# Induced-set attention and squared-ReLU MLP on one core: scores read in a burst, batch 0 transposed on TensorE, the weights' chain in one PSUM bank

## The chip, the cores and the metric

The kernel runs on one core of a Trainium2 chip. The metric is the time of one execution in microseconds (us); of several runs the median counts. PE is TensorE (matmuls; PEld its weight loads), DVE is VectorE, ACT is ScalarE, POOL is GpSimd, and SP issues the DMAs. Each engine works through its own instructions in the order that was fixed when the program was built, and waits in place for what an instruction needs.

## What is computed

```python
x: (4, 12480, 128); inducing: (32, 128); w_in: (128, 2048); w_out: (2048, 128)   # weights arrive as float64
def mab(q, kv):
    s = scale * (q @ kv.T);  a = softmax(s, -1);  return a @ kv
h = mab(inducing, x)          # 32 rows look at all 12480 rows of a batch
y = mab(x, h)                 # 12480 rows look at the 32 rows of h
out = relu(y @ w_in) ** 2 @ w_out
```

## The kernel before

Four batches (b = 0 to 3) of 12480 rows are each cut into seven groups G (six of 1920 rows, one of 960) and into 26 chunks of 480 rows; four chunks make a group. All tiles hold features or the 32 inducing rows on partitions.

**First attention, `first(b)`.** For each group, `scores` (L264) multiplies the transposed rows `xp` (loaded from `xT` by `load_xT`, L259) with the inducing rows into PSUM; DVE scales them into `sT` and keeps the maximum (L298). When all seven groups are there, a global maximum is made (L305 to L316), ACT takes the exponential (L323), DVE transposes it 32x32-wise into `en` (L333), and PE multiplies `en` with the rows themselves, `xnb`, loaded from `xn` in halves of a group (L283 to L287), into `hacc` (L345). Every group has its own `hacc` in PSUM, which DVE adds into `hq` (L351, L353). Two small matmuls (L360, L361) and L363 to L365 give `hT`, the 32 attended rows.

**Second attention, `second(b, G)`.** `scores` again, now with `hT`; DVE transposes out of PSUM into `e` (L381) and takes the maximum (L383), POOL subtracts it (L387), ACT takes the exponential (L388), DVE sums (L391 to L393), POOL divides (L394), DVE transposes back (L397), and the weights `a` are written as two halves of float16 to DRAM (`ad`, L408) and loaded back in another layout as `dT` (L428). `squares(b, G)` (L442 to L454) makes 32 further squared features, which land in rows 96 to 127 of `dT` (`zz`, four DMAs a group).

**The MLP by pairs.** Each row of y is a mix of 32 rows of h, so relu(y @ w_in) squared is written with 512 squared differences of the mixing weights. `Chunk.up` (L638) multiplies `dT` with the constant `pairs` into `hp`, `lift` squares it on ACT (L647) into `g`, `down` multiplies `g` with the batch's weights `w16` (L653) and `dT` with `lin` (L654) into `po`, and `o = po * osc + bias` goes out on ACT (L657) or DVE (L659), whichever has less work held against it (`to_act`), and by DMA to `outT` (L660). Three `o` tiles exist.

**The weights of a batch, `prepare(b)`.** A chain from `hT`: `hw` = h @ w_in, some forty small DVE operations, `products(c)` (DVE, L518, four tiles G) and `sums(c)` (16 matmuls each, L527; evacuated into `w16` by ACT, L175, or DVE, L179), `R` (L534), `cat` (L580 to L582), `w4` (L606, into `lin`). Each of its PSUM results takes the one buffer of `side_psum`, so that each waits until the one before has been read. The four `sums` must all be evacuated before the first chunk of the batch can be finished.

**The start.** The weights are read as pairs of 32-bit words and made float32 on DVE by `narrow` (L236 to L242): `w_in` in four pieces of seven operations, then `w_out` in four (`wo`, L224). Between them stand the first attention of batch 0, `prepare(0)` with `second(0, 0)` and `second(0, 1)`; then the chunks begin.

**Order.** During the chunks a list `plan` says at which chunk each step of the next batches' generators is recorded: `spread(gen, steps, start, length)`, with constants (`PACE`, `MOST`, `EARLY`, `LONG`, `LAG`, `WEIGHTS`). `background(k)` runs what is due. The framework then moves instructions on each engine by a model of its own; what stands in the program is shown below under the change. The pool of `xp` tiles has NX = 9 buffers, that of `xnb` XB = 5, the PSUM of scores and squares (`att_psum`) and of the chain (`side_psum`) one each. A fallback behind `tc.If` at the end is not executed.

## Time and profile before

| | us |
|---|---|
| median of 3 runs (lowest to highest) | 462.41 (461.12 to 466.04) |
| the profiled execution | 464.73 |
| its span | 463.0 |
| first chunk's `hp` on PE | 86.1 |
| last ACT square of the last chunk | 454.5 |

The span runs from the first to the last instruction of the profiled execution. The profile gives busy time per engine; a window view gives the same for any stretch, in order: length, PE, PEld, DVE, ACT, POOL (each busy us and number of instructions), granted TensorE clock, share of the DMA engines, GB/s. A window view of one line gives that line's engine alone. The timeline gives start, duration, engine, line, output <- inputs and count of merged instructions, and in brackets the engine's idle time before with what released it. "The chain that ended last" goes back from the last instruction to what released each step. A float32 matmul stands as two in the trace (x8 for four), a float32 transpose through PE as one. Weight loads show stationary shapes as 128\*32.

### The profile page before, as it was taken

The numbers are of one execution on the slowest core, as the hardware profiler recorded it, in microseconds if no ns is written. First come the engines' busy times: TensorE is split into PE (matmuls) and PEld (weight loads), VectorE is DVE, ScalarE is ACT, GpSimd is POOL, SyncE is SP. The second block draws the span as 40 slices with busy tenths as digits, with TensorE's granted clock in tenths as the row PEclk, the third lists the DMA queues.
The fourth block names the chain that finished last, engine by engine and source line by source line (L and its number), as shares of the span: only waits on it lengthen the run. The fifth ranks groups of instructions, "written<-read, shape, count | busy, mean of one in ns | idle before, by whom it ended". The sixth has DMA issues, their size and how long they took to land.

```text
span 463.0 us, 8566 instructions
## 1 busy us (share of the span) xinstructions
PE 366.8 (79%) x2979; PEld 163.2 (35%) x2979; DVE 325.7 (70%) x902; ACT 282.0 (61%) x397; POOL 85.9 (19%) x93
## 2 busy tenths in 40 slices
PE   0644744899979889878789888988879898788994
PEld 0003413543335333333244234433433344343441
DVE  8969378685643199497561899689626999996442
ACT  1004123479994497437567798566666878067993
POOL 1000011141210030232200132144100423340000
PEclk9999975699979799799599999999999999999998
DMA  7999980377759983667889958644794354337432
GB/s 296 421 248 392 372 295 24 97 240 249 207 173 337 335 277 101 197 188 187 266 276 293 344 195 244 195 138 145 240 290 154 102 167 165 101 128 231 151 136 105
DMA packets 64771, 100.71 MB, mean 218 GB/s; under 512 B 22992, under 2 KB 53968, under 8 KB 64720
## 3 DMA queue, kind: packets, MB, share of 16 engines
q1 hardware_dynamic: 64720, 100.09, 66.3%
q8 instruction: 25, 0.41, 0.4%
q14 instruction: 26, 0.21, 0.1%
HBM read 64.91 MB, written 31.95 MB: 209 GB/s over the span
## 4 chain that ended last, share of the span: by engine, by line
PE 30%; DVE 28%; DMA 26%; ACT 6%; issue 5%; SPq 2%; POOL 1%; ACTq 0%; DVEq 0%; POOLq 0%
DMA xnb<-xn_dram 8%; PE hp L638 8%; PE po L653 7%; ACT g L647 5%; DMA outT_dram<-o 5%; PE s L264 4%; PE hacc L345 4%; DMA xp_False<-xT_dram 4%; DMA dT<-zz 3%; DVE o L659 3%; DVE G L518 3%; DVE a L407 2%; PE wq L527 2%; DMA wo<-w_out_dram 2%; DMA dT<-ad 2%
## 5 line engine op out<-in xcount | busy, mean ns | idle before, releaser
L647 ACT ACTIVATE g<-hp 128x960 f16<-128x960 f32 x208 | 194.4, 974 | 60.7 <-PE hp L638 48.2
L638 PE MATMUL hp<-dT,pairs 96*128 96x480 f16 x416 | 121.4, 381 | 7.3 <-ACT g L647 4.9
L653 PE MATMUL po<-g,w 128*128 128x480 f16 x416 | 115.8, 377 | 7.6 <-ACT o L657 3.4
L387 POOL TENSOR_TENSOR e<-e,mx 128x480 f32<-128x480 f32 (+1 forms) x28 | 28.0, 999 | 232.2 <-DVE mx L383 76.3
L659 DVE TENSOR_SCALAR o<-po,osc,bias 128x480 f32<-128x480 f32 x60 | 45.4, 763 | 30.5 <-PE po L654 17.8
L653 PEld LDWEIGHTS <-w 128*128 128x128 f16 x416 | 40.6, 100 | 60.7 <-issue 19.3
L638 PEld LDWEIGHTS <-pairs 96*128 96x128 f16 x416 | 35.8, 101 | 66.6 <-issue 42.1
L345 PE MATMUL hacc<-xnb,en 128*32 128x128 f32 x784 | 38.3, 324 | 16.8 <-DMA xnb<-xn_dram 8.7
L264 PE MATMUL s<-xp_False,indT_sb 128*32 128x480 f32 (+1 forms) x224 | 32.9, 665 | 22.4 <-DMA xp_False<-xT_dram 12.1
L654 PE MATMUL po<-dT,lin 128*128 128x480 f16 x104 | 39.1, 379 | 7.7 <-DMA dT<-zz 7.5
L452 POOL TENSOR_TENSOR zz<-z 128x480 f16<-128x480 f32 (+1 forms) x28 | 30.2, 1078 | 66.3 <-DVE z L448 39.8
L323 ACT ACTIVATE sT<-sT,nb 128x480 f32<-128x480 f32 (+1 forms) x28 | 18.2, 658 | 33.5 <-DVE nb L316 33.5
L394 POOL TENSOR_TENSOR e<-e,z 128x480 f32<-128x480 f32 (+1 forms) x28 | 27.0, 967 | 56.1 <-DVE z L393 36.9
L345 PEld LDWEIGHTS hacc<-xnb,en 128*32 128x32 f32 x784 | 24.4, 126 | 33.6 <-DMA xnb<-xn_dram 9.7
L657 ACT ACTIVATE o<-po,bias,osc 128x480 f32<-128x480 f32 x44 | 33.0, 762 | 5.2 <-DMA outT_dram<-o 4.4
L353 DVE TENSOR_TENSOR hq<-hacc,hq 128x128 f32<-128x128 f32 x24 | 7.0, 291 | 37.6 <-PE hacc L345 37.6
L264 PE MATMUL s<-xp_False,hT 128*32 128x480 f32 (+1 forms) x224 | 27.7, 563 | 4.3 <-DVE k L195 1.4
L448 DVE TENSOR_SCALAR z<-sq,off,cut 128x480 f32<-128x480 f32 (+1 forms) x28 | 21.5, 767 | 9.3 <-PE sq L442 9.3
L518 DVE TENSOR_TENSOR G<-hwp,hw 128x512 f16<-128x512 f16 x64 | 24.9, 455 | 4.1 <-PE wq L527 4.1
L388 ACT ACTIVATE e<-e 128x480 f32<-128x480 f32 (+1 forms) x28 | 16.2, 578 | 17.0 <-POOL e L387 17.0
L404 ACT ACTIVATE a<-a,lessen 128x480 f16<-128x480 f32 (+1 forms) x20 | 13.6, 681 | 16.5 <-DVE a L397 16.3
L298 DVE TENSOR_SCALAR_CACHE_REDUCE sT<-s 128x480 f32<-128x480 f32 (+1 forms) x28 | 17.0, 608 | 9.1 <-PE s L264 9.1
(190 smaller groups left out, 419.2 us busy)
## 6 DMA issues: line engine op xcount, KB each, us to landing
outT_dram<-o SPq DMA_DIRECT2D x104, 240.0 KB, 2.8
xp_False<-xT_dram SPq DMA_DIRECT2D x24, 960.0 KB, 6.8
xnb<-xn_dram SPq DMA_DIRECT2D x28, 448.0 KB, 5.2
xnb<-xn_dram SPq DMA_DIRECT2D x24, 512.0 KB, 5.9
dT<-ad SPq DMA_DIRECT2D x72, 120.0 KB, 2.6
ad<-a SPq DMA_DIRECT2D x24, 240.0 KB, 2.5
dT<-zz SPq DMA_DIRECT2D x104, 30.0 KB, 2.3
wi<-w_in_dram SPq DMA_DIRECT2D x4, 512.0 KB, 5.6
```

What stands on the lines that cost most here:

```text
L264: nc.tensor.matmul(ps[32 * q:32 * q + 32, 0:w], lhsT, xp[:, w * q:w * q + w], start=True, stop=True,)
L345: st.last = nc.tensor.matmul(hacc[32 * q:32 * q + 32, 0:P], en[:, t], xg[:, t % 8], start=t < 4, stop=t + 4 >= nb32,)
L387: nc.gpsimd.tensor_tensor(e[:, 0:t], e[:, 0:t], mx[:, 0:t].unsqueeze(2).broadcast_to([P, t, MI]), op=ALU.subtract)
L394: nc.gpsimd.tensor_tensor(e[:, 0:t], e[:, 0:t], z[:, 0:t].unsqueeze(2).broadcast_to([P, t, MI]), op=ALU.mult)
L452: nc.gpsimd.tensor_tensor(g[rows], zv[rows], zv[rows], op=ALU.mult)
L518: tt(g[:, :, MI * j:MI * j + n], hwp[:, :, 0:n], hw16f[:, :, s0:s0 + n], op=ALU.mult)
L638: nc.tensor.matmul(hp[:, i, 0:CH].rearrange("p (q t) -> p q t", q=4), pairs[0:96, (2 * j + i) * P:(2 * j + i + 1) * P], self.dT[0:96], sta ...
L647: nc.scalar.activation(self.g[:, 2 * j:2 * j + 2], self.hp.pop(j)[:, 0:2, 0:CH], AF.Square)
L653: nc.tensor.matmul(po[:, 0:CH], st.w16[:, i], self.g[:, i], start=i == 0, stop=False)
L654: done = [nc.tensor.matmul(po[:, 0:CH].rearrange("p (q t) -> p q t", q=4), st.lin, self.dT, start=False, stop=True)]
L657: nc.scalar.activation(o, po[:, 0:CH], AF.Identity, bias=st.bias, scale=st.osc)
L659: done.append(nc.vector.tensor_scalar(o, po[:, 0:CH], st.osc, st.bias, op0=ALU.mult, op1=ALU.add))
```

## The change

Nothing in the results is changed. There are five parts.

1. **Batch 0 is read once.** `xT` of batch 0 is no longer loaded. All 13 halves of batch 0's rows are loaded at the start into five `xnb` tiles, four slices of a new tile `scored`, two G tiles and two tiles of the start pool. `turn(G)` transposes each 128x128 block on PE against `ident` into `two_banks` PSUM (15 blocks a group), and ACT copies the halves into the `xp` tile. The same halves serve `hacc`. `words` has 4 buffers instead of 6.
2. **One `hacc` per batch.** PE sums all groups in one PSUM bank; the six adds into `hq` go.
3. **The second scores in a burst.** `second` writes its transposed scores into one of eight slots of `scored` and yields right after; the plan runs this first step of all groups close together (`READ`), the other steps at their own pace (`REST`). The following batch's `xp` loads are due right after the reads (`NX` 9 to 7), and its `first` and `prepare` are due earlier (batch 3's `head` 53.6 chunks instead of 61, batch 1's 10.8 instead of 13.9).
4. **The weights' chain** uses one `bank` of PSUM in slices, its small matmuls are regrouped, all four `sums` go side by side into one `wq`, are evacuated by ACT alone, and one reduction takes their maximum. `w4` comes ahead of the sums. `prepare_w_out` and the squares use the `po` pool.
5. **Batch 0's later groups** (2 to 6) are read in the start; their further steps are held behind the mark `bias` of `prepare(0)`. Evacuation of `o`: on ACT for the 18 chunks after each `head` (`heavy`) and the last chunk, on DVE otherwise (66 on ACT and 38 on DVE, before 44 and 60).

```diff
-NX = 9
+NX = 7
+HEAVY = 18
-MOST = 17
-PACE = (1.2, 2, 2, 3)
-EARLY = -1
+SLOTS = 8
+READ = (0, 2, 1, 1)
+REST = 2.6
...
+        def turn(G):
+            w = WID[G]
+            xp = st.xp[G] = flow.tile([P, 4 * CH], F32, tag="xp", name=f"xp_{b}_{G}", bufs=NX)[:, 0:4 * w]
+            to = xp.rearrange("p (q n) -> p q n", q=4)
+            for h in range(2 * G, min(2 * G + 2, HALVES)):
+                k = 8 - h % 2
+                ps = two_banks(f"xt_{h}").rearrange("p a (t c) -> p (a t) c", c=P)
+                for t in range(k):
+                    nc.tensor.transpose(ps[:, t], xns[h][:, t], ident)
+                whole = k if h < HALVES - 1 else 7
+                c0 = 256 * (h % 2)
+                nc.scalar.copy(
+                    to[:, :, c0:c0 + 32 * whole].rearrange("p q (t r) -> p t q r", r=32),
+                    ps[:, 0:whole].rearrange("p t (q r) -> p t q r", q=4),
+                )
...
-            hacc = side_psum(f"hacc_{b}_{G}")
+            hacc = hacc or side_psum(f"hacc_{b}")
...
-            if G == 0:
+            if G == NG - 1:
                 nc.vector.tensor_copy(hq[:, 0:P], hacc[:, 0:P])
-            else:
-                nc.vector.tensor_tensor(hq[:, 0:P], hacc[:, 0:P], hq[:, 0:P], op=ALU.add)
...
-        e = work.tile([P, 15, MI], F32, tag="e2", name=f"e2_{b}_{G}")
+            k = 480 * ((NG * b + G) % SLOTS)
+            e = scored[:, k:k + 480].rearrange("p (t i) -> p t i", i=MI)
         nc.vector.transpose(ef[:, 0:wb], ps[:, 0:wb])
+        yield
...
-            ps = side_psum(f"wq_{b}_{c}")
             for k in range(NF):
-                nc.tensor.matmul(ps[:, 0:P], g[:, k], w_hi[:, k], start=k == 0, stop=k == NF - 1)
-            evac(st.w16[:, c], ps[:, 0:P], P, tsg[:, c:c + 1])
-            nc.vector.tensor_reduce(wm[:, c:c + 1], ps[:, 0:P], axis=AX.X, op=ALU.max, apply_absolute_value=True)
+                last = nc.tensor.matmul(wq[:, c * P:c * P + P], g[:, k], w_hi[:, k], start=k == 0, stop=k == NF - 1)
+            nc.scalar.mul(st.w16[:, c], wq[:, c * P:c * P + P], tsg[:, c:c + 1])
...
-    for G in range(NG):
-        sts[0].xp[G] = load_xT(0, G)
+    sts[0].rows = {h: load_half(0, h, homes[h]) for h in range(HALVES)}
...
             for G in range(NG):
-                free = max(0, G + NG - NX)
-                start = max(reads[b - 1, free] + 0.6, EARLY if b == 1 else -9)
+                start = reads[b - 1, G] + 0.4
                 spread(loads(b, G), 1, start, 0)
-                spread(sums, 1, start + 3, 0)
-            start += 3.5
+                start = max(start + 2.5, 26 * (b - 2) + 7 + 1.4 * G)
+                spread(sums, 1, start, 0)
+            start += 1
             spread(sums, 18, start, LONG)
-            head = max(start + LONG + LAG, 26 * b - MOST)
+            head = max(start + LONG + LAG, 26 * (b - 1) + 0.6)
             spread(prepare(b), 19, head, WEIGHTS)
...
-                spread(second(b, G), 4, reads[b, G], 2)
+                spread(gen, 1, reads[b, G], 0)
+                spread(gen if b else behind(gen, lambda: sts[0].marks), 4, rest, 2)
...
-                done = chunks[n - 1].down()
+                done += chunks[n - 1].down(heavy(n - 1))
```

**PE at the very start.** `s_0_G` are the first scores of batch 0's group G, `xt` the transposed blocks, `place` and `rows` further homes of the halves. Before:

```order
L264 MATMUL s_0_0_220<-xp_0_False,indT_sb 32x480 x4
L264 MATMUL s_0_1_236<-xp_1_False,indT_sb 32x480 x4
L264 MATMUL s_0_2_242<-xp_2_False,indT_sb 32x480 x4
L264 MATMUL s_0_3_258<-xp_3_False,indT_sb 32x480 x4
L264 MATMUL s_0_4_264<-xp_4_False,indT_sb 32x480 x4
L264 MATMUL s_0_5_290<-xp_5_False,indT_sb 32x480 x4
L264 MATMUL s_0_6_296<-xp_6_False,indT_sb 32x240 x4
```

and now:

```order
L302 MATMUL xt_230<-ident,xnb_164 128x128 x8
L302 MATMUL xt_240<-ident,xnb_165 128x128 x7
L302 MATMUL xt_266<-ident,xnb_166 128x128 x8
L278 MATMUL s_0_0_249<-xp_0_229,indT_sb 32x480 x4
L302 MATMUL xt_276<-ident,xnb_167 128x128 x7
L302 MATMUL xt_292<-ident,xnb_168 128x128 x8
L278 MATMUL s_0_1_285<-xp_1_265,indT_sb 32x480 x4
L302 MATMUL xt_302<-ident,scored 128x128 x7
L302 MATMUL xt_328<-ident,scored 128x128 x8
L278 MATMUL s_0_2_311<-xp_2_291,indT_sb 32x480 x4
```

Each group's scores now stand behind 15 transposes, one half ahead of the scores that need them.

**DVE between the last `en` tiles and `hT` of batch 0.** `no` is the narrowing of `w_out`. Before:

```order
L333 STREAM_TRANSPOSE en_4_455<-sT_217 128x480
L353 TENSOR_TENSOR hq_332<-hacc_3_432,hq_332 128x128
L333 STREAM_TRANSPOSE en_5_475<-sT_217 128x480
L353 TENSOR_TENSOR hq_332<-hacc_4_458,hq_332 128x128
L333 STREAM_TRANSPOSE en_6_494<-sT_217 128x256
L272 MEMSET sT_967 128x16
L353 TENSOR_TENSOR hq_332<-hacc_5_477,hq_332 128x128
L353 TENSOR_TENSOR hq_332<-hacc_6_496,hq_332 128x128
L363 TENSOR_SCALAR zr_512<-hs_509 128x32
```

and now:

```order
L243 TENSOR_SCALAR no_m<-wo_394 128x512
L357 STREAM_TRANSPOSE en_4_572<-sT_226 128x480
L244 SCALAR_TENSOR_TENSOR wo_sb<-no_m,no_r 128x512
L357 STREAM_TRANSPOSE en_5_590<-sT_226 128x480
L357 STREAM_TRANSPOSE en_6_607<-sT_226 128x256
L286 MEMSET sT_1004 128x16
L375 COPY hq_468<-hacc_482 128x128
L197 TENSOR_SCALAR inv_t<-wsum 128x1
```

No operation of DVE stands between the `en` tiles any more that waits for PE; one copy of the whole sum follows the last.

**DVE at the change from batch 2 to batch 3.** Before, from the `bias` of batch 3 (chunk 78 is its first; `w_1_151` is its `w16`, `o_0`, `o_1` are its first outputs):

```order
L518 TENSOR_TENSOR G_2_4187<-hwp_4032,hw_3_3959 128x16x32 x4
L406 TENSOR_SCALAR a_3_3_4484<-a_3_3_4482,lessen 128x480
L529 TENSOR_REDUCE wm_4034<-wq_0_4168 128x1
L381 STREAM_TRANSPOSE e_3_4_4543<-s_3_4_4538 128x480
L407 SCALAR_TENSOR_TENSOR a_3_3_4484<-a_3_3_4482,lessen,a_3_3_4484 128x480
L410 TENSOR_TENSOR least_d<-least_d,a_3_3_4484 128x480
L383 TENSOR_REDUCE mx_3_4_4545<-e_3_4_4543 128x15
L179 TENSOR_SCALAR w_1_151<-wq_1_4201,tsg 128x128
...
L179 TENSOR_SCALAR w_1_151<-wq_3_4322,tsg 128x128
...
L659 TENSOR_SCALAR o_0_4706<-po_0_4700,osc_157,bias_158 128x480
```

and now (`o_21` to `o_25` are the last outputs of batch 2):

```order
L683 TENSOR_SCALAR o_21_4626<-po_21_4620,osc_146,bias_147 128x480
L544 TENSOR_TENSOR G_2_4078<-hwp_3872,hw_3_3803 128x16x32 x4
L433 SCALAR_TENSOR_TENSOR a_3_6_4550<-a_3_6_4548,lessen,a_3_6_4550 128x240
L436 TENSOR_TENSOR least_d<-least_d,a_3_6_4550 128x240
L683 TENSOR_SCALAR o_22_4644<-po_22_4638,osc_146,bias_147 128x480
L732 TENSOR_REDUCE dmin<-least_d 128x1
L544 TENSOR_TENSOR G_3_4118<-hwp_3872,hw_3_3803 128x16x32 x3
...
L683 TENSOR_SCALAR o_25_4715<-po_25_4709,osc_146,bias_147 128x480
...
L683 TENSOR_SCALAR o_0_4733<-po_0_4727,osc_157,bias_158 128x480
```

The last products and the last group's weights of batch 3 stood between outputs of batch 2 and of batch 3; now they stand four chunks ahead of the end of batch 2. At the change from batch 0 to batch 1 the four sums still stand on PE among the first four `hp` of batch 1, as before, but four of the seven second scores of batch 1 that stood among them stand ahead of them now.

More of the change, by code (lines that the diff above doesn't have):

```diff
@@ L293, in first @@
                 xns = {h: load_xn(h) for h in range(XB)}
+            if not b:
+                turn(G)
             ps = att_psum(f"s1_{b}_{G}")
@@ L301, in first @@
             yield
-        xns = xns or {h: load_xn(h) for h in range(XB)}
         m1 = small("m1")
@@ L536, in prepare @@
             )
-        cat = st.cat
-        rm = small("rm")
-        nc.vector.tensor_reduce(rm, ps[:, 0:P], axis=AX.X, op=ALU.max, apply_absolute_value=True)
-        nc.vector.tensor_copy(cat[:, 0:P], ps[:, 0:P])
-        yield
-        products(0)
-        products(1)
-        bp = side_psum(f"pl_{b}")
-        nc.tensor.matmul(bp[:, 0:1], before, inc[:, NF - 1:NF], start=True, stop=True)
-        nc.tensor.matmul(bp[0:1, 2:3], inc[:, NF - 1:NF], onec[:, 0:1], start=True, stop=True)
-        nc.tensor.matmul(bp[:, 4:5], every, rm, start=True, stop=True)
         pl, tl, t = small("pl"), small("tl"), small("t")
@@ L554, in prepare @@
         ts(flags[:, b:b + 1], bp[0:1, 2:3], MX + 0.5, None, op0=ALU.is_le)
+        yield
+        bp2 = bank[:, 136:152]
+        for k in range(NF):
+            q = k % 4
+            nc.tensor.matmul(
+                bp2[32 * q:32 * q + 32, 0:MX], hws[:, k], hot[:, k], start=k < 4, stop=k >= NF - 4,
+            )
+        cat = st.cat
+        rm = small("rm")
+        nc.vector.tensor_reduce(rm, ps[:, 0:P], axis=AX.X, op=ALU.max, apply_absolute_value=True)
+        nc.vector.tensor_copy(cat[:, 0:P], ps[:, 0:P])
+        nc.vector.tensor_copy(cat[:, P + 16:P + MI], bp2[:, 0:MX])
+        cs = work.tile([P, 4, MI], F32, tag="cs", name=f"cs_{b}")
+        nc.vector.tensor_copy(cs, cat[:, P:P + MI].unsqueeze(1).broadcast_to([P, 4, MI]))
+        yield
+        nc.tensor.matmul(bp[:, 4:5], every, rm, start=True, stop=True)
+        ps = bank[:, 160:424]
+        rep4 = rep.rearrange("p q i -> p (q i)")
+        nc.tensor.matmul(ps[0:96, 0:P + MI], rep4[:, 0:96], cat, start=True, stop=True)
+        nc.tensor.matmul(ps[:, 256:257], cs.rearrange("p j r -> p (j r)"), part, start=True, stop=True)
+        nc.tensor.matmul(ps[:, 260:261], cat[:, 0:P], onec[:, 0:1], start=True, stop=True)
         ts(tl, bp[:, 4:5], 2.0 ** -60, None, op0=ALU.max)
@@ L603, in prepare @@
         nc.scalar.copy(g4[:, :, 16:MI], hot)
-        ps = side_psum(f"w4_{b}")
         for k in range(NF):
-            nc.tensor.matmul(ps[96:P, 0:P], g4[:, k], w_hi[:, k], start=k == 0, stop=k == NF - 1)
-        ts(st.lin[96:P], ps[96:P, 0:P], t[96:P], None, op0=ALU.mult)
+            nc.tensor.matmul(bank[96:P, 0:P], g4[:, k], w_hi[:, k], start=k == 0, stop=k == NF - 1)
+        ts(st.lin[96:P], bank[96:P, 0:P], t[96:P], None, op0=ALU.mult)
+        products(1)
+        wq = side_psum(f"wq_{b}")
+        sums(0)
         yield
+        products(2)
+        sums(1)
+        yield
+        products(3)
         sums(2)
         yield
-        sums(3)
-        nc.vector.tensor_reduce(cm2[:, 1:2], wm, axis=AX.X, op=ALU.max)
+        last = sums(3)
+        st.ends = last, nc.vector.tensor_reduce(cm2[:, 1:2], wq, axis=AX.X, op=ALU.max, apply_absolute_value=True)
         ts(cm2[:, 1:2], cm2[:, 1:2], inv_t, None, op0=ALU.mult)
@@ L708, in smallest, with heavy @@
         yield
-    plan = []
+    plan, busy = [], []
+    def heavy(n):
+        return any(a <= n < z for a, z in busy)
     def spread(gen, steps, start, length):
@@ L714, in spread, with behind @@
             plan.append((start + length * n / steps, len(plan), gen))
+    def behind(gen, marks):
+        while True:
+            with ExitStack() as held_back:
+                for i in marks():
+                    held_back.enter_context(tc.issue_after(i.ins))
+                if next(gen, gen) is gen:
+                    return
+            yield
     def loads(b, G):
@@ L753, in background @@
             due = next(todo, None)
-    soon = chain(second(0, 0), second(0, 1))
+    soon = chain(scored_by[0, 0], scored_by[0, 1])
     for n, _ in enumerate(prepare(0)):
-        if n == 3:
+        if n == 0:
             prepare_w_out()
@@ L769, in attend_then_relu2_mlp @@
         for j in (0, 1):
-            chunk.lift(j)
+            done = [chunk.lift(j)]
             if nxt:
```

111 lines of the change are left out of this document (57 added, 54 removed).

## The prediction

> **What bounds the kernel now.** I read the busy times, then the chain that ended last, then windows.
>
> ```profile
> PE 366.8 (79%) x2979; PEld 163.2 (35%) x2979; DVE 325.7 (70%) x902; ACT 282.0 (61%) x397; POOL 85.9 (19%) x93
> 8.19 17.83 DMA xp_False<-xT_dram
> 38.54 9.12 DMA xnb<-xn_dram
> 59.62 1.11 PE hw L264 x8
> 86.15 1.71 PE hp L638 x4
> ```
>
> No engine is full over the whole. The chain (last four rows) shows three stages: until 59.6 us transfers and DVE make batch 0's `hT`; until 86.2 the weights' chain runs and no chunk does; then 104 chunks. In the third stage I count ACT's squares, two to a chunk, per stretch (first number in parentheses), and look at the engines where they stop:
>
> ```profile
> 190.00:200.00 10.00, 4.32 (x5) 0.80 0.56 165
> 200.00:210.00 10.00, 0.00 (x0) 1.00 0.54 164
> 380.00:390.00 10.00, 8.59 (x10) 1.00 0.43 138
> 390.00:400.00 10.00, 2.46 (x3) 0.83 0.55 174
> 400.00:410.00 10.00, 1.83 (x2) 1.00 0.28 75
> 410.00:420.00 10.00, 8.53 (x10) 1.00 0.51 166
> 440.00:450.00 10.00, 9.89 (x12) 1.00 0.39 139
> 330.00:350.00 20.00, 16.80 (x191) 8.11 (x182) 6.58 (x17) 12.23 (x15) 0.00 (x0) 1.00 0.94 299
> 360.00:390.00 30.00, 27.37 (x203) 12.02 (x202) 30.00 (x79) 24.60 (x32) 9.37 (x9) 1.00 0.40 126
> 390.00:410.00 20.00, 15.27 (x142) 7.94 (x141) 18.90 (x53) 5.92 (x9) 7.10 (x8) 0.91 0.41 125
> ```
>
> Undisturbed at the end, 12 squares pass in 10 us. At 200 to 210 none passes, at 390 to 410 five. These are the changes to batch 1 and batch 3: the new batch's first outputs wait for its four sums, and these for DVE, which is 18.9 of 20 us busy with the batch's products and last groups. Sixty us earlier (330 to 350) DVE was busy 6.58 of 20. So the chunks' stage is bound by work that comes at the wrong time, PE being next to full elsewhere.
>
> **The change part by part.** *The start.* Its end was set by DVE:
>
> ```profile
> 8.82 0.42 DVE L236 TENSOR_SCALAR ni_a<-wi 128x512 uint32<-128x512 uint32 x1
> 12.62 0.42 DVE L236 TENSOR_SCALAR ni_a<-wi 128x512 uint32<-128x512 uint32 x1
> 31.60 0.40 DVE L298 TENSOR_SCALAR_CACHE_REDUCE sT<-s 128x240 f32<-128x240 f32 x1
> 47.71 1.07 PE L345 MATMUL hacc<-xnb,en 128*32 128x128 f32 x14 [2.76 <-DMA xnb<-xn_dram]
> 54.02 0.43 DVE L333 STREAM_TRANSPOSE en<-sT 128x256 f32<-128x256 f32 x1
> 59.37 0.19 DVE L365 TENSOR_TENSOR hT<-hs,zr 128x32 f32<-128x32 f32 x1
> ```
>
> One `narrow` takes 3.8 us (first two rows). From the last scores (32.0) to `hT` (59.6) passed 27.6 us, with DVE waiting for `hacc`, which waited for rows. Now the rows lie there. Between the last scores and `hT` the new DVE order has 3.2 narrowings (12.2), seven `en` (six of 0.67 and 0.43: 4.5) and small operations (1.3), 18 us, then the last `hacc`, one copy, two small matmuls and three operations (2.8, from 56.6 to 59.4 before): 20.8. If the last scores are in at 32 again, `hT` is there at 52.8 instead of 59.6: 6.8 earlier. Whether they are is up to PE:
>
> ```profile
> 12.11 1.83 PE L264 MATMUL s<-xp_False,indT_sb 128*32 128x480 f32 x8 [12.11 <-DMA xp_False<-xT_dram]
> 60.50 0.99 PE L264 MATMUL s<-xp_False,hT 128*32 128x480 f32 x8
> 58.09 0.30 PEld L360 LDWEIGHTS hs<-z,every 128*128 128x128 f32 x2 [0.89 <-DVE hq L353]
> 75.00 0.50 PEld L546 LDWEIGHTS pl<-inc,before 128*128 128x128 f32 x2 [2.53 <-issue]
> L617 PE MATMUL cm<-ident,cm 128*1 128x128 f32 x12 | 2.4, 271 | 0.0
> 99.53 0.49 PE L617 MATMUL cm<-ident,cm 128*1 128x128 f32 x3
> ```
>
> The same scores take 1.83 us early and 0.99 later; PE runs at half speed at the start (the clock column, which reads 1.00 there, does not show it) and had sped up by 58 us, after ten us of dense `hacc`. No 128x128 block is transposed before. Its weight load is like one of L360 or L546: 0.15 us fast, 0.25 slow; the matmul behind it adds 0.11 ((0.49 - 0.27) / 2) if loads overlap it, and its whole 0.27 if nothing overlaps. So a block costs 0.15 to 0.52, 98 blocks 15 to 51 us. I take 0.15 from the second group on, since PE has no gap any more: a group is 15 x 0.15 + 0.99 = 3.2 us, and six and a half groups from 10 us on, the first two at 5.6 (15 x 0.25 + 1.83), end at 10 + 11.2 + 4.5 x 3.2 = 36: 4 later than before. ACT's 13 copies of up to 1024 columns (like L647, 974 ns for 960) fill 13 of some 26 us.
>
> ```profile
> 60.00:75.00 15.00, 5.86 (x60) 2.60 (x53) 13.72 (x49) 5.42 (x8) 2.17 (x2) 0.65 0.49 177
> 75.00:90.00 15.00, 9.91 (x94) 6.78 (x95) 9.90 (x40) 4.79 (x8) 2.94 (x3) 0.56 0.29 84
> ```
>
> From `hT` to the first `hp` DVE is busy nearly throughout. The squaring chain stays; the new order puts ahead of the first `hp` five transposes of scores (3.2), three maxima (1.9) and one sum (0.65), 5.75 in all, of which some 3 fall into the 6.4 us that DVE was idle in these 30. The 26.5 us become about 29.5. Together: -6.8 + 4 + 3 = 0, between -6 (PE no bound, more of the new work in idle time) and the two cases below that PE makes.
>
> *What the start took over.* Five second scores and one first score leave the chunks' stage: six times 0.99 on PE, six reads of 0.65 on DVE. PE is near full there: -4, between 0 and -6. The chunks need the moved groups no earlier, and the yields that hold their other steps back are after the bias, so nothing new waits.
>
> *The change to batch 3.* The four sums, `w4` and the last groups' steps now stand before chunk 78. Five squares passed in 20 us; at ten in 10 us (the stretches on both sides) they take 5: 15 us free. The work itself goes to earlier chunks, and what it costs there is PE's part, since DVE has 13 free us at 330 to 350:
>
> ```profile
> 392.15 1.86 PE L527 MATMUL wq<-w_hi,G 128*128 128x128 f16 x16 [0.61 <-DVE bias L591]
> 396.85 1.05 PE L527 MATMUL wq<-w_hi,G 128*128 128x128 f16 x16
> 399.16 1.07 PE L606 MATMUL w<-w_hi,g 128*32 128x128 f16 x16
> ```
>
> Four sums, one `w4` and three scores at about 1 us are 8 us of PE; half of it finds PE idle (it is busy 16.8 of 20 there): 4 back. -11, between -15 and 0 (all of it lands where PE is full or DVE late).
>
> *The change to batch 1.* The sums still stand among chunks 26 to 29, but the second scores do not, and the chain starts three chunks earlier. Of the 10 us without a square I give back half: -5, between -10 and 0.
>
> *DVE's load.*
>
> ```profile
> L659 DVE TENSOR_SCALAR o<-po,osc,bias 128x480 f32<-128x480 f32 x60 | 45.4, 763 | 30.5 <-PE po L654 17.8
> L657 ACT ACTIVATE o<-po,bias,osc 128x480 f32<-128x480 f32 x44 | 33.0, 762 | 5.2 <-DMA outT_dram<-o 4.4
> L353 DVE TENSOR_TENSOR hq<-hacc,hq 128x128 f32<-128x128 f32 x24 | 7.0, 291 | 37.6 <-PE hacc L345 37.6
> ```
>
> 22 outputs of 0.76 and 24 additions of 0.29 leave DVE (24 us), 22 outputs come to ACT (17). Where DVE is full (360 to 390), ACT has 5 us free in 30, and PE 2.6. So -3, between -6 and +4 (ACT's squares queue behind outputs that wait for `po`). The three reductions less of `wq` and the single bank are inside these.
>
> *Loads.* The start reads 6.4 MB less: `xT` goes, and the rows' halves take its place. Three more of batch 1's `xp` loads issue before the first chunk, where the DMA engines are at 0.29 to 0.49 (rows above). SP reaches batch 0's `dT` loads only after batch 1's `xp` 0 to 5, each of which waits for its own reading score; these are done long before the bias, so 0.
>
> Sum: 0 - 4 - 11 - 5 - 3 = -23. The profiled execution had a span of 463.0 and took 464.7 us; the median of the runs shown is 462.4, 0.6 below the span. The span comes to 440, the median to **439 us**. The ends of the terms add up to -43 and +4; half-way to them on both sides the likeliest case spans 429 to 452.
>
> **The rivals.**
>
> *PE stays slow through the transposes.* For it: in the first 31 us the scores kept PE busy some 60% of the time and it stayed at half speed. Against it: it had sped up by 58 us, when `hacc` had filled it to 84%. Then a group costs 5.6 us and the last scores come at 10 + 6.5 x 5.6 = 46, 10 later than reckoned: **449 us**. The Trainium skill ("TensorE: Matmul & The Clock Gate", Part 4: PE-mode transpose) says that transposes do not count as activity for the clock gate, so that full speed does not set in; by that rule this case would hold. No trace here shows a stretch of such transposes.
>
> *The moved work costs where it lands what it saves.* For it: PE is 91% busy at 360 to 390, and the stages of `hacc` are bound by transfers (DMA share 0.94 at 330 to 350), so that work put there delays them. Then only the -4 of the start's extra work remains: **458 us**, within 1%.
>
> *Transposes without overlap make the start longer than the chunks gain.* One mechanism: each block's load (0.25) and matmul (0.27) in a row, 0.52. A group is 15 x 0.52 + 1.83 = 9.6 us, the last scores come at 10 + 6.5 x 9.6 = 72, 36 later than reckoned, which the gain of 23 does not cover: **475 us**, slower. It decides from the block time that makes them 23 late: ((59 - 10) / 6.5 - 1.83) / 15 = 0.38 us. For it: nothing in the trace shows such loads hidden behind such matmuls. Against it: L617's three took 0.49 together, not 0.81.
>
> **How the numbers follow.** The likeliest case has 0.52, the slow clock 0.20, the cancelling 0.15, the long start 0.13. A measurement of this kernel tells about 1% from no change, that is 457.8 to 467.0. Faster by more: the first two, 0.72. Same: 0.15. Slower: 0.13. The range leaves out the long start and what lies under the likeliest case's own range by more than 5: 424 to 460.
>
> **What would show it.** First `hp` at 82 to 88 us in the new profile, the first scores at about 1 us from the third group on and not 1.83, blocks at 0.15 us; no window of 10 us at the change to batch 3 with fewer than five squares, and a tail of some 26 chunks at about 12 squares in 10 us; at the change to batch 1 still a gap, of some 5 us; DVE near 295 us busy, ACT near 318. The prediction is wrong if the first `hp` comes after 95 us, or if the squares pass more slowly in the middle (130 to 350) than before, where 5 to 6 passed in 10 us.

## The result, and the profile after

The changed kernel takes 437.2 us (median of 4 runs, 435.8 to 440.5), the kernel before beside it 461.8 (461.1 to 466.0): ratio 0.946, 95% interval 0.938 to 0.954. 439 was forecast. The profiled execution is the longest of the four, 440.5 us with a span of 438.7, against 464.7 and 463.0 before. The sum was -23 us and the span fell by 24.3, but the parts of the sum did not come out as written. Runs more than 1.5% above the fastest of their kernel are left out of the ratios, here and below, but not out of the medians.

The engines' busy times, from the page of the changed kernel:

```profile
PE 366.6 (84%) x3077; PEld 173.7 (40%) x3077; DVE 312.3 (71%) x830; ACT 312.3 (71%) x444; POOL 87.7 (20%) x93
```

DVE lost 13.4 us and not 30, ACT gained 30.3.

To see where the time came from I take from the trace when the first square of a chunk starts on ACT; the last row is the end of the last square. All times are in us. The lengths that the expectations below quote were read from windows of 2 us and differ from these by up to 2 us.

| chunk | before | changed | | length of | before | changed | difference |
|---|---|---|---|---|---|---|---|
| 0 | 87.1 | 88.3 | | start | 87.1 | 88.3 | +1.2 |
| 26 | 187.5 | 189.2 | | batch 0 | 100.4 | 100.9 | +0.5 |
| 52 | 299.1 | 287.6 | | batch 1 | 111.6 | 98.4 | -13.2 |
| 78 | 387.0 | 380.2 | | batch 2 | 87.9 | 92.6 | +4.7 |
| end | 455.4 | 431.4 | | batch 3 | 68.4 | 51.2 | -17.2 |

The start and batch 0 gave nothing. Batches 1 and 3 gave all of it. Two spans matter: chunks 26 to 36 fell from 55.9 to 39.5 us, chunks 78 to 84 from 28.1 to 11.8. The change to batch 3 in windows of the squares' line (length, busy time and count, clock, DMA share, GB/s):

```profile
370.00:380.00 10.00, 5.79 (x7) 1.00 0.48 155
380.00:390.00 10.00, 8.91 (x10) 1.00 0.50 154
390.00:400.00 10.00, 9.27 (x11) 1.00 0.55 162
400.00:410.00 10.00, 9.17 (x11) 1.00 0.69 224
```

The two windows with 2.46 and 1.83 that stood here before are gone. The counts take a square that lies in two windows twice. By their starts, ten squares fall into each of the last three windows; the "12 in 10 us" that the prediction read in 440 to 450 of the kernel before are eleven, and the changed kernel's last batch ran at ten.

The start, from the timeline of TensorE (PE) in the changed kernel (start, length, line, tiles, count):

```profile
11.14 5.14 PE L302 MATMUL xt<-ident,xnb 128*128 128x128 f32 x23 [11.14 <-DMA xnb<-xn_dram]
16.21 1.14 PE L278 MATMUL s<-xp,indT_sb 128*32 128x480 f32 x8
17.29 1.86 PE L302 MATMUL xt<-ident,xnb 128*128 128x128 f32 x15
19.27 1.01 PE L278 MATMUL s<-xp,indT_sb 128*32 128x480 f32 x8
```

A block took 0.22 us at first and 0.124 from 17 us on (0.25 and 0.15 were assumed), and the scores between them 1.14 and then 1.01, where they took 1.83 before. The further way to the first `hp`: `hT` in DVE's timeline, then three rows of the chain that ended last.

```profile
53.11 0.19 DVE L386 TENSOR_TENSOR hT<-hs,zr 128x32 f32<-128x32 f32 x1
```

```profile
72.62 6.28 DMA ad<-a
79.79 6.80 DMA dT<-ad
87.32 1.71 PE hp L662 x4
```

`hT` is there 6.3 us earlier than before (59.37), but from it to the first `hp` pass 34 us instead of 27, and the last 15 of them are two transfers.

What the start did bring shows in the later batches. Their `hT`, in DVE's timeline of before and of the changed kernel:

```profile
156.88 0.19 DVE L365 TENSOR_TENSOR hT<-hs,zr 128x32 f32<-128x32 f32 x1
253.13 0.19 DVE L365 TENSOR_TENSOR hT<-hs,zr 128x32 f32<-128x32 f32 x1
349.23 0.19 DVE L365 TENSOR_TENSOR hT<-hs,zr 128x32 f32<-128x32 f32 x1
```

```profile
138.99 0.19 DVE L386 TENSOR_TENSOR hT<-hs,zr 128x32 f32<-128x32 f32 x1
233.97 0.19 DVE L386 TENSOR_TENSOR hT<-hs,zr 128x32 f32<-128x32 f32 x1
322.91 0.19 DVE L386 TENSOR_TENSOR hT<-hs,zr 128x32 f32<-128x32 f32 x1
```

Each is 18 to 26 us earlier. The plan's numbers moved the chains of batches 1 and 3 by three and seven chunks (some 11 and 27 us at 3.7 us a chunk) and that of batch 2 hardly at all (35.2 chunks for 35), so at least batch 2's 19 us come from elsewhere. The first scores of batch 1 begin at 81.7 us instead of 101.6. So the question for the experiments is which part of the change brings the later batches forward, and why batch 0 has nothing of its lighter load.

### The profile page after: what moved, and what is told of

It is laid out like the page before. It is cut to its first block, busy times and chain, and to the rows that moved or that the text cites. A ratio compares the mean times of both kernels' runs of the same rounds, so it can differ in the third digit from the quotient of the medians.

```text
span 438.7 us, 8759 instructions
## 1 busy us (share of the span) xinstructions
PE 366.6 (84%) x3077; PEld 173.7 (40%) x3077; DVE 312.3 (71%) x830; ACT 312.3 (71%) x444; POOL 87.7 (20%) x93
## 4 chain that ended last, share of the span: by engine, by line
PE 45%; DVE 30%; DMA 15%; ACT 5%; issue 3%; SPq 1%; POOL 0%; DVEq 0%; ACTq 0%
PE hp L662 14%; PE po L677 13%; DMA xnb<-xn_dram 6%; PE hacc L369 5%; PE s L278 4%; ACT g L671 3%; PE wq L552 3%; PE po L678 3%; DVE G L544 3%; DMA rows<-xn_dram 3%; DVE scored L406 2%; DMA outT_dram<-o 2%; DVE z L417 2%; DMA ad<-a 2%; DVE mx L409 2%
## 5 line engine op out<-in xcount | busy, mean ns | idle before, releaser
L681 ACT ACTIVATE o<-po,bias,osc 128x480 f32<-128x480 f32 x66 | 49.9, 760 | 7.5 <-DMA outT_dram<-o 4.0
L683 DVE TENSOR_SCALAR o<-po,osc,bias 128x480 f32<-128x480 f32 x38 | 29.5, 776 | 35.5 <-PE po L678 30.1
L413 POOL TENSOR_TENSOR scored<-scored,mx 128x480 f32<-128x480 f32 (+1 forms) x28 | 29.6, 1063 | 113.0 <-DVE k L198 57.0
L369 PE MATMUL hacc<-xnb,en 128*32 128x128 f32 x664 | 28.3, 298 | 12.4 <-DMA xnb<-xn_dram 9.3
L420 POOL TENSOR_TENSOR scored<-scored,z 128x480 f32<-128x480 f32 (+1 forms) x28 | 29.1, 1042 | 39.1 <-DVE z L419 18.5
L357 DVE STREAM_TRANSPOSE en<-sT 128x480 f32<-128x480 f32 (+1 forms) x28 | 17.8, 640 | 22.3 <-PE hacc L369 19.7
L414 ACT ACTIVATE scored<-scored 128x480 f32<-128x480 f32 (+1 forms) x28 | 16.3, 584 | 12.4 <-POOL scored L413 12.4
L305 ACT COPY xp<-xt 128x896 f32<-128x896 f32 (+1 forms) x13 | 12.3, 956 | 17.5 <-PE xt L302 17.5
L278 PE MATMUL s<-xp_False,hT 128*32 128x480 f32 (+1 forms) x168 | 21.0, 574 | 4.3 <-DVE sT L322 3.3
L278 PE MATMUL s<-xp_False,indT_sb 128*32 128x480 f32 (+1 forms) x168 | 21.0, 568 | 3.4 <-DVE scored L406 2.2
```

Of the source, the lines that this page charges most:

```text
L278: nc.tensor.matmul(ps[32 * q:32 * q + 32, 0:w], lhsT, xp[:, w * q:w * q + w], start=True, stop=True,)
L369: st.last = nc.tensor.matmul(hacc[32 * q:32 * q + 32, 0:P], en[:, t], xg[:, t % 8], start=G == 0 and t < 4, stop=G == NG - 1 and t + 4 >= ...
L413: nc.gpsimd.tensor_tensor(e[:, 0:t], e[:, 0:t], mx[:, 0:t].unsqueeze(2).broadcast_to([P, t, MI]), op=ALU.subtract)
L420: nc.gpsimd.tensor_tensor(e[:, 0:t], e[:, 0:t], z[:, 0:t].unsqueeze(2).broadcast_to([P, t, MI]), op=ALU.mult)
L681: done.append(nc.scalar.activation(o, po[:, 0:CH], AF.Identity, bias=st.bias, scale=st.osc))
L683: done.append(nc.vector.tensor_scalar(o, po[:, 0:CH], st.osc, st.bias, op0=ALU.mult, op1=ALU.add))
```

## The experiments

The kernel before ran beside each group on the same chip. Its median there lay between 461.6 and 467.3, so kernels of different groups are compared by their ratio to it.

### Batch 3's chain at chunk 61 again

```diff
-            head = max(start + LONG + LAG, 26 * (b - 1) + 0.6)
+            head = max(start + LONG + LAG, 61 if b == 3 else 26 * (b - 1) + 0.6)
```

> The changed kernel (437.2 us) with one number put back: the weights' chain of batch 3 begins at chunk 61 again and not at 53.6; everything else is the change's. Theory 'place': the 16 us that batch 3 gained come from the sums and last groups standing ahead of chunk 78. Then chunks 78 to 84 take some 25 to 29 us again (13.6 in the changed kernel, 29.2 before), the chunks of batch 2 run up to 3 us faster, and the time is 447 to 450 us. Rival 'load': the gain comes from DVE having less to do (outputs on ACT, no additions of hq), wherever the chain stands. Then the time stays within 3 us of 437, and chunks 78 to 84 under 18 us.

Measured 432.2 us, ratio 0.936 (0.924 to 0.948); chunks 78 to 84 took 12.0 us. But the edit did not do what its theory needed: in TensorE's order the four sums of batch 3 stand behind the `hp` of 75, 76, 77 and 78 chunks, exactly as in the changed kernel. The framework takes the plan's number as a wish; `hT`, at 317 us, came later than chunk 61 would have asked for. So this says that the number is not what moves the chain, and nothing about what a late chain costs.

### Batch 1's chain at chunk 13.9 again

```diff
-READ = (0, 2, 1, 1)
+READ = (0, 1.5, 1, 1)
...
-            head = max(start + LONG + LAG, 26 * (b - 1) + 0.6)
+            head = max(start + LONG + LAG, 13.9 if b == 1 else 26 * (b - 1) + 0.6)
```

> The changed kernel with batch 1's chain of weights beginning at chunk 13.9 as before and not at 10.8 (its second scores at a pace of 1.5 chunks and not 2, so that batch 2's work stands where the change has it). Theory 'place': the 14.7 us that batch 1 gained (chunks 26 to 36 took 38.6 us, before 57.0) come from the chain's three chunks, and batch 0's zero is the price of it. Then chunks 26 to 36 take 47 to 55 us, chunks 0 to 26 some 4 us less than 100.9, and the time is 442 to 447. Rival 'load': the gain is DVE's and ACT's shares, and three chunks do not matter: 435 to 440 us, chunks 26 to 36 under 43.

Measured 436.3 us, ratio 0.943 (0.933 to 0.952). Chunks 26 to 36 took 43.3 us, 4 more, and chunks 0 to 26 98.3, 3 less: what the one gains the other pays. The sums of batch 1 did not come later in the order (25 to 28, before this edit 26.5 to 29.5), because here too the number was not what held them. What moved is the second scores' pace.

### The outputs shared as before

```diff
-            if act:
+            if to_act(220 + 0.833 * CH, 110 + 1.042 * CH):
```

> The changed kernel with the outputs o shared between DVE and ACT by the running sums of planned load, as before, and not by the stretches called heavy. Theory 'place' (the prediction's own term for DVE's load was -3 us): the time is 437 to 441, and the change of batch 3 (chunks 78 to 84) stays under 18 us. Rival 'load': DVE is the one that the batches' changes wait for, and it gets 10 to 20 outputs of 0.76 us back in just those stretches: 446 to 452 us, with chunks 78 to 84 over 20 us.

Measured 439.4 us, ratio 0.949 (0.938 to 0.961), 2 us more than the changed kernel by medians. That agrees with the prediction's -3, but the intervals do not tell it from nothing. The old rule puts 53 outputs on DVE here, not the 60 of before. Chunks 78 to 84 took 17.6 us, 6 more than in the changed kernel, with batch 3's sums at 79 to 82 in TensorE's order. So this part does help to bring them ahead, but it is not the 17 us.

### Batch 1's loads behind batch 0's first `dT`

```diff
-                spread(loads(b, G), 1, start, 0)
+                gen = loads(b, G)
+                spread(behind(gen, lambda: [dT_read]) if b == 1 and G > 2 else gen, 1, start, 0)
```

`dT_read` is the last of the three DMAs of batch 0's first `dT`.

> The changed kernel with the loads of batch 1's xp 3 to 6 issued behind batch 0's first dT load and not ahead of it. Theory 'contention': the 1 MB loads slow the round trip of batch 0's a and dT (from a's store to the first hp passed 14.7 us, before 7.0), which is why the first hp came at 87.3 us although hT came 6.3 us earlier. Then the round trip takes 8 to 10 us, the first hp comes at 82 to 84, and the time is 432 to 435. Rival 'DVE's chain': the first hp is set by the bias and the weights (the order of DVE), and the round trip only fills that time: first hp at 86 to 88 and 436 to 439 us. Third possibility: the start gains and batch 1's scores, now later, lose it again before chunk 36.

Measured 430.5 us, ratio 0.929 (0.919 to 0.939). The queue of the DMA issues (SP) of the changed kernel and of this one, then the first `hp` here:

```profile
72.62 1.81 SPq L434 DMA_DIRECT2D ad<-a  x2
76.04 0.34 SPq L273 DMA_DIRECT2D xp_False<-xT_dram  x1
78.92 2.84 SPq L454 DMA_DIRECT2D dT<-ad  x6
```

```profile
72.38 1.61 SPq L434 DMA_DIRECT2D ad<-a  x2
74.97 1.29 SPq L454 DMA_DIRECT2D dT<-ad  x3
76.36 1.33 SPq L273 DMA_DIRECT2D xp_False<-xT_dram  x3
79.31 1.66 PE L662 MATMUL hp<-dT,pairs 96*128 96x480 f16 x4
```

`a` is stored at the same time, but the load that has to wait for it goes out after 2.6 us instead of 6.3, and `hp` starts at 79.3. In three kernels with the changed kernel's start (the first three experiments) it started at 83.8, 83.9 and 83.4, so the 87.3 of the changed kernel's profile holds some 3.5 us in which its `dT` landed late, which none of these three repeats; the loads in the way cost another 4.4. Those on the way with `a` and `dT` are batch 1's `xp` 4 and 5, issued at 72.20 and 76.04 us in the changed kernel and landed 5.6 and 9.5 us later. The median time from issue to landing (last column) of the loads issued from 74 to 85 us, in the changed kernel and in the first experiment:

```profile
dT<-ad SPq DMA_DIRECT2D x6, 120.0 KB, 6.7
```

```profile
dT<-ad SPq DMA_DIRECT2D x6, 120.0 KB, 3.8
```

"Contention" holds, and this experiment's own trace shows it once more: the three `dT` loads issued just ahead of the `xp` loads landed after 2.4 to 2.8 us, the three behind them after 10.0 to 10.4.

That the earlier start is what shortens the whole is not shown. The profiled execution, the longest of the four (435.3 us), had lost its head start by chunk 36: chunks 20 to 24 took 27.5 us instead of 19.4, chunk 26 began at 195.7 us (189.2 in the changed kernel) and chunk 36 at 229.3 (228.7), as the third possibility had it. Its span is 5.2 us shorter by what batch 2 took, 87.9 us for 92.6.

### Batch 0's `xp` loaded again

```diff
-                turn(G)
...
+    for G in range(NG):
+        sts[0].xp[G] = load_xT(0, G)
     sts[0].rows = {h: load_half(0, h, homes[h]) for h in range(HALVES)}
```

> The changed kernel, but batch 0's xp is loaded from xT again, seven loads ahead of the rows, and nothing is transposed on TensorE. This undoes the part of the change at the start. Theory 'rows': hT came 6.3 us earlier only because the rows for hacc are there when DVE is ready; with 7 MB more ahead of them hT comes at 59 to 65 us (53.1 in the changed kernel), the first hp at 89 to 95, and the time is 441 to 448. Rival 'the start does not set the time': what the start gains is lost again in batch 0, as the profile of the changed kernel suggests (batch 0 took 100.9 us, before 99.3), and the time stays within 435 to 440.

Measured 448.3 us, ratio 0.967 (0.959 to 0.976): some 10 us. The theory named the right size and the wrong way. `hT` came earlier, not later; late is what is loaded after the rows, `w_out`. DVE's timeline, `hT` and the last operation of each of the four narrowings of `w_out`:

```profile
49.52 0.18 DVE L386 TENSOR_TENSOR hT<-hs,zr 128x32 f32<-128x32 f32 x1
49.95 0.69 DVE L244 SCALAR_TENSOR_TENSOR wo_sb<-no_m,no_r 128x512 f32<-128x512 uint32 x1
56.56 0.68 DVE L244 SCALAR_TENSOR_TENSOR wo_sb<-no_m,no_r 128x512 f32<-128x512 uint32 x1
66.96 0.68 DVE L244 SCALAR_TENSOR_TENSOR wo_sb<-no_m,no_r 128x512 f32<-128x512 uint32 x1
80.08 0.68 DVE L244 SCALAR_TENSOR_TENSOR wo_sb<-no_m,no_r 128x512 f32<-128x512 uint32 x1
...
93.53 0.14 DVE L616 TENSOR_SCALAR bias<-bias 128x1 f32<-128x1 f32 x1
```

In the changed kernel the third narrowing ended at 44.7 and the last at 49.3, all ahead of `hT`, and `bias` stood at 77.6. Here three of them lie among the steps of the weights' chain, and `bias` comes 16 us later. The first `hp` still started at 87.5, since it needs neither; but chunks 0 to 4 took 26.3 us instead of 14.5. So what the transposes are worth, with all rows loaded in the start, is the 6.4 MB that do not stand ahead of `w_out`. The kernel before had no such delay: its narrowings ended at 33.4 to 47.2 us, with five buffers for the halves of the rows where the new start has thirteen homes. The 10 us are therefore a cost that the new start avoids, not a gain over the old one.

### `hacc` per group again

```diff
-            hacc = hacc or side_psum(f"hacc_{b}")
+            hacc = side_psum(f"hacc_{b}_{G}")
...
-            if G == NG - 1:
-                nc.vector.tensor_copy(hq[:, 0:P], hacc[:, 0:P])
+            if G == 0:
+                nc.vector.tensor_copy(hq[:, 0:P], hacc[:, 0:P])
+            else:
+                nc.vector.tensor_tensor(hq[:, 0:P], hacc[:, 0:P], hq[:, 0:P], op=ALU.add)
```

> The changed kernel with hacc one PSUM tile per group again, added into hq on DVE (24 additions of 0.29 us back). Theory 'in the shade': these stretches are bound by transfers (DMA share 0.9 to 1.0) and the additions cost 0 to 2 us: 436 to 440. Rival 'DVE': each addition waits for its hacc at the head of DVE's queue, as it did before (37.6 us of idle time stood ahead of the 24), so that outputs and reads behind it are late: 444 us or more, with batch 0 to 2 each some 2 us longer.

Measured 441.5 us, ratio 0.950 (0.943 to 0.958), 0.4% above the changed kernel's, within the intervals. In the start `hT` came at 56.7 instead of 53.1; batches 0 to 2 took 104.6, 93.4 and 95.4 us (100.9, 98.4, 92.6). "In the shade" is nearer.

### The weights' chain in its old form

```diff
-            spread(prepare(b), 19, head, WEIGHTS)
+            spread(prepare_old(b), 19, head, WEIGHTS)
```

`prepare_old` is the function of the kernel before, word for word but for the mark; it serves batches 1 to 3, batch 0 keeps the new form.

> The changed kernel with the weights' chain of batches 1 to 3 in its form from before (four PSUM tiles for the sums and one for each small step, products 0 and 1 early, the sums shared between DVE and ACT with a maximum after each); batch 0's chain is the change's. The first runs showed that where the chain begins matters little: with 61 for 53.6 the chunks 78 to 84 took 13.3 us. Theory 'chain's form': the sums were late before because each waited for a PSUM tile and for DVE between them. Then chunks 78 to 84 take 20 to 29 us again, chunks 26 to 36 50 us or more, and the time is 447 to 455. Rival 'reads': the form is worth nothing, 436 to 441 us.

Measured 434.3 us, ratio 0.939 (0.932 to 0.946); chunks 78 to 84 took 14.6 us, chunks 26 to 36 37.5. The chain's form is worth nothing by itself. Its sums stand at 73.5 to 79.5 in the order.

### The old pace of the second scores

```diff
-READ = (0, 2, 1, 1)
-REST = 2.6
+READ = (0, 2, 2, 3)
+REST = 0
```

> The changed kernel with the pace of the second scores as before: each group's score is read and worked on at once, 2, 2 and 3 chunks apart in batches 1, 2 and 3, instead of a burst of reads with the rest 2.6 chunks apart. Batch 3's next loads and its chain follow the reads and begin at chunk 59.6. Theory 'reads': before, the last groups of batch 3 stood at chunks 72 to 80, in DVE's queue among the products of the chain; with them back, chunks 78 to 84 take 20 to 29 us (13.6 in the changed kernel, 29.2 before) and the time is 445 to 452. Rival 'chain's form': the pace is worth nothing, 435 to 441 us, chunks 78 to 84 under 17.

Measured 432.8 us, ratio 0.931 (0.923 to 0.939), chunks 78 to 84 11.8 us. The burst of batches 1 to 3 is worth nothing either; rather, it costs up to 1.6%, by intervals that just meet (0.938 and 0.939).

### Five parts back together

The edits of the outputs, `hacc`, the chain and the pace above, and the squares' sums in the scores' tile:

```diff
-        ps = ps_o.tile([P, 512], F32, tag="po", name=f"sq_{b}_{G}")
+        ps = att_psum(f"sq_{b}_{G}")
```

> The changed kernel with five parts put back at once, four of which cost nothing singly: outputs shared by the running sums, hacc per group with additions, the weights' chain of batches 1 to 3 in its old form, the old pace of second scores, and the squares' sums in the PSUM tile of the scores. What is left of the change: the start with transposed rows, batch 0's scores read there, the kept score tiles and the plan's numbers. Theory 'relief': each of these parts alone takes enough off DVE or off the one PSUM tile to bring batch 3's four sums ahead of chunk 78, and only all together put them behind it (in the order of TensorE they now stand at the 82nd chunk's hp, as before; 75 to 78 in the changed kernel). Then chunks 78 to 84 take 22 to 29 us (13.6) and the time is 445 to 452. Rival 'pipeline': the gain comes from every batch's first pass beginning 20 us earlier (first scores of batch 1 at 82 us, before 102), which these parts do not touch: chunks 78 to 84 under 18 us, 434 to 441.

Measured 475.2 us (469.1 to 480.4), the kernel before beside it 461.6 (454.3 to 464.9): slower than before, by 3% of the medians. The change to batch 3 in windows of the squares:

```profile
390.00:400.00 10.00, 5.61 (x6) 0.93 0.55 187
400.00:410.00 10.00, 0.00 (x0) 0.67 0.49 137
410.00:420.00 10.00, 1.54 (x2) 0.72 0.14 38
```

The stall of before is back (chunks 78 to 84 took 34.3 us), and two more came with it (chunks 20 to 24 took 30.9 us, 52 to 56 21.4; 19.4 and 15.3 in the changed kernel). The first scores of batch 1 began at 103.2 us, so this kernel, for all that it reads batch 0's scores in the start, had lost the 20 us of head start. Neither theory had said so: "pipeline" held these parts for harmless to the first pass.

### The squares in the scores' tile, alone

The last diff by itself.

> The changed kernel with one part put back: the squares' sums sq of each group use the one PSUM tile of the scores again and not the pair of the outputs. With this and four other parts put back the kernel took 475 us, and the first scores of batch 1 then came at 103 us and not at 82. Theory 'single tile': this part alone does most of that, since first scores, second scores and squares take turns on one tile, each turn ending with a read on DVE: first scores of batch 1 after 95 us, 448 us or more, chunks 78 to 84 over 20 us. Rival 'redundant reliefs': none of the five costs much alone, as the other four have shown; then 434 to 442 us, with chunks 78 to 84 under 18 us, and what made 475 is that none of the five was left.

Measured 451.5 us, ratio 0.977 (0.965 to 0.988): 3.2% above the changed kernel's, 14 us, with intervals apart. The first scores of batch 1, in TensorE's timeline of this kernel and, behind it, of the changed one:

```profile
98.34 1.01 PE L278 MATMUL s<-xp_False,indT_sb 128*32 128x480 f32 x8
```

```profile
81.68 1.01 PE L278 MATMUL s<-xp_False,indT_sb 128*32 128x480 f32 x8
```

17 us later, by a tile. `att_psum` is one tile; first scores, second scores and squares take it in turn, and every turn ends with DVE reading it. "Single tile" holds, but for the place of the loss: chunks 78 to 84 took 11.8 us, and chunks 52 to 60 44.9 instead of 29.8. There the last first scores of batch 3 and the squares of batch 2 take turns on the tile, TensorE reaches the outputs' `po` behind them, and ACT stands 4.1 us before it; the seven exponentials of the next first pass come next, and no square starts between 296.4 and 308.1 us. Rows of TensorE and ACT, then the squares' window:

```profile
298.28 0.61 PE L278 MATMUL s<-xp_False,indT_sb 128*32 128x240 f32 x8 [0.32 <-DVE z L474]
300.83 0.39 PE L468 MATMUL sq<-dT,singles 96*32 96x480 f16 x4 [0.41 <-DVE z L474]
301.35 0.36 PE L678 MATMUL po<-dT,lin 128*128 128x480 f16 x1
301.75 0.75 ACT L681 ACTIVATE o<-po,bias,osc 128x480 f32<-128x480 f32 x1 [4.14 <-PE po L678]
```

```profile
300.00:310.00 10.00, 1.80 (x2) 0.83 0.33 82
```

The delay begins in the start: batch 0's third second score comes at 81.2 us, behind the first squares (77.5), where the changed kernel has it at 61.0. Batch 1's `xp` loads wait for these scores, so they were not in the way here: the first `dT` loads landed after 2.6 us and the first `hp` started at 78.0. So the chunks' stage lost more than the 14 us.

### Batch 1's first pass held back

```diff
             sums = first(b)
+            if b == 1:
+                sums = behind(sums, lambda: [sts[0].hp])
...
-                start = max(start + 2.5, 26 * (b - 2) + 7 + 1.4 * G)
+                start = max(start + 2.5, 26 * (b - 2) + 7 + 1.4 * G, 4 + 0.4 * G if b == 1 else -9)
```

`sts[0].hp` is the latest `hp` matmul of batch 0, so this edit binds where the plan's numbers did not.

> The changed kernel with the whole first pass of batch 1 held back behind the hp of chunks 4 to 6, as far back as before (first scores from 102 us on and not from 82). Theory 'pipeline': each batch's hT hangs on the first pass of its batch, and this on the batch before it; so hT of batch 1 comes some 16 us later (139 in the changed kernel, 157 before), the sums of batch 1 come after chunk 28 again, chunks 26 to 36 take 50 us or more (38.6), and the time is 445 to 455. Rival 'relief': there is slack of some 10 us between hT and the sums, and what the later first pass costs is got back from batch 0's chunks, which have less beside them: chunks 0 to 26 some 4 to 8 us faster, chunks 26 to 36 under 44, 433 to 440 us.

Measured 442.9 us (439.4 to 444.9) beside 461.6 of the kernel before, a ratio of medians of 0.959, 1.4% above the changed kernel's ratio; there is no interval for it. The first scores of batch 1 began at 96.4 and its `hT` came at 147.6. Chunks 26 to 36 took 34.9 us, fewer than in the changed kernel, but chunks 20 to 24 took 31.8 instead of 19.4:

```profile
170.00:180.00 10.00, 0.00 (x0) 0.54 0.66 194
```

A late first pass seems to cost, so "relief" is wrong about the slack; and the loss is not where "pipeline" had it, since the order now has the sums of batch 1 at 24.5 to 27.5.

### Both good edits together

The edits of batch 1's loads and of the old pace.

> The changed kernel with two of the earlier edits together: batch 1's loads of xp 3 to 6 behind batch 0's first dT load, and the second scores at the old pace, which alone gave 430.5 and 432.8 us. If the two act in different places (the start; the changes between batches) their gains over the changed kernel's 437.2 add: 426 to 431 us, first hp at 79 to 81 us. If the pace's gain was only a better landing of dT by chance, the time is that of the first edit alone, 429 to 433 us.

Measured 442.9 us, ratio 0.955 (0.944 to 0.966): the gains do not add, the two together are no better than the changed kernel. The first `hp` came at 79.5, as hoped, and chunks 20 to 24 took 31.8 us. The stall there is not the pair's alone: it was 27.5 and 27.4 us in the profiles of the two single edits. TensorE's timeline there, with the idle time and what ended it in brackets:

```profile
167.30 1.01 PE L278 MATMUL s<-xp_False,indT_sb 128*32 128x480 f32 x8 [1.05 <-DVE scored L406]
171.24 1.83 PE L278 MATMUL s<-xp_False,hT 128*32 128x480 f32 x8 [2.93 <-DVE sT L322]
174.36 1.83 PE L278 MATMUL s<-xp_False,indT_sb 128*32 128x480 f32 x8 [1.30 <-DVE scored L406]
175.99 1.59 PE L623 MATMUL bank<-w_hi,g 128*32 128x128 f16 x13
```

and the squares' window:

```profile
170.00:180.00 10.00, 0.62 (x1) 0.55 0.64 174
```

First scores of batch 2 and second scores of batch 1 alternate on the one tile. Each waits at the head of TensorE's queue until DVE has read the one before, DVE has some ten operations of the weights' chain and of `a` between two reads, and the chunks' matmuls stand behind. That is the stall in its pure form: not the sums, but the scores ahead of them.

Best of all kernels run is the one with batch 1's loads behind `dT`, 430.5 us; its interval just meets the changed kernel's, and the two did not run side by side.

## Why the prediction came out, step by step

The forecast of 439 us lies 2 us from the median, but the terms behind it were up to 14 us off and cancelled: batches 0 and 2 became 5 us longer where -4 was forecast, and batches 1 and 3 gave 30 where 16 were. So that the sum agrees this closely is luck; that the gain lies at the changes to batches 1 and 3 was foreseen.

**The start, 0.** +1.2 us in the profiled execution, about -2.5 where `dT` landed as usual. Two errors cancelled. The last scores and `hT` were better than said (18.7 us between them for 20.8, and blocks of 0.124 us instead of 0.15), which made `hT` 6.3 us earlier and not 2.8. The way from `hT` to `hp` was worse: 30.8 us in the first experiment, 29.5 forecast, and 34 in the changed kernel's own profile.

**Loads, 0.** This step failed. The prediction asked whether SP would come late to the loads of `dT` because of a wait for a reading score, and that did not set the time: they waited for `a` to land. It didn't ask what loads of up to 1 MB do to the two small transfers beside them. Those were the end of the start, and holding the loads back took 4.4 us off the first `hp`.

**Transposes.** That they would overlap and that TensorE would speed up was right, and both rivals about them fell. But the price of 98 blocks was the wrong thing to look at: what loading `xT` beside all the rows would cost, by the kernel that does it, is 10 us through `w_out`, which was no term of the sum.

**Work taken over, -4.** Batch 0 became 0.5 us longer. The six scores left it, but the earlier first pass brought batch 1's second scores and batch 2's first scores into it: of batch 2's seven first scores five now begin ahead of chunk 26, where three did, and of batch 1's seven second scores all, where three did. That this is the reason is argued from the two traces. The experiment that held the first pass back did not show it, since a stall came at chunk 20 there; the one with the pace of 1.5 agrees, with 3 us less in batch 0 and 4 more behind it.

**The changes to batches 1 and 3, -5 and -11.** They were -13.2 and -17.2, with 4.7 given back in batch 2. The place is right and the mechanism half: the sums do stand ahead of chunk 78 now. The cause was put to the plan's numbers ("the four sums and the last groups' steps now stand before chunk 78"), and the numbers don't bind. What moves batch 1's first pass is when the one scores' tile comes free. The step that is missing in the prediction is the one line that moves the squares out of that tile: it gave it no price, and alone it is worth 14 us. Batch 3's 17 us hang on no single part: chunks 78 to 84 took 11.5 to 17.6 us in every experiment with one or two edits, the tile's too, and 34.3 only with five.

**DVE's load, -3.** The kernel with the old sharing agrees with the size (+2), within the noise. The count was wrong: 22 outputs and 24 additions did go, but DVE lost 13.4 us and not 24. The same operations took longer, here before and in the changed kernel:

```profile
L410 DVE TENSOR_TENSOR least_d<-least_d,a 128x480 f16<-128x480 f16 x24 | 10.3, 431 | 0.0
```

```profile
L436 DVE TENSOR_TENSOR least_d<-least_d,a 128x480 f16<-128x480 f16 x24 | 14.3, 595 | 0.0
```

Why was not tried.

**The rival "moved work costs where it lands what it saves"** holds for batch 0 and for several parts taken singly: `hacc`, the chain's form, the burst and the plan's numbers each moved the time by 1.6% at most, some of them in the wrong direction. Yet with four of them and the tile undone together the kernel was 38 us slower than the changed one, by medians, and the tile accounts for 14. So they replace each other: each of the four can be missed while the others stand, and with none of them left the stall is back. Whether one alone would do, or which pair, was not run and stays open.

## What to carry to other kernels

Price every line of a diff that moves a tile from one PSUM pool to another: a pool with one buffer is a queue, and what waits in it waits at the head of an engine that runs in order. Before crediting a schedule's number, look whether the instruction moved in the engine's order; two of the numbers here did not bind. And where a stage ends in a small transfer that others wait for, look at what large loads were issued just ahead of it.

## What the runs showed of the hardware

TensorE sped up on transposes alone: it had stood until 11.14 us, did nothing but transposes for 5 us, and the next scores took 1.14 and 1.01 us where they take 1.83 at half speed; the blocks themselves went from 0.22 to 0.124. In the first experiment's trace the change falls among the transposes themselves: blocks started every 0.213 us from 10.87 us on and every 0.109 from 13.8, and the first scores only followed at 15.07. By the rule that the Trainium skill states ("TensorE: Matmul & The Clock Gate", Part 4: PE-mode transpose), that transposes don't count as activity, this would not have happened; the measurement decides, for transposes made as here, by matmul against an identity in float32.

It also slows down inside one stall. In the rows of the last experiment the scores at 167.30, behind a wait of 1.05 us, still took 1.01; those at 171.24, behind a further wait of 2.93 us, took 1.83, at a granted clock of 0.55 in that window of 10 us. So a stall at the head of TensorE's queue costs its own length and the half speed after it.

The first `dT` loads, 120 KB each, took 6.7 us to land behind the 1 MB loads in the changed kernel's execution and 3.5 to 4.4 in seven others with the same loads ahead (2.6 before, where fewer of those loads were on the way). That is 3 us on the way to the first chunk, against a spread of 4.7 between the four runs of the changed kernel (435.8 to 440.5).
